# Attention tables, value products and result transfers moved to other places in a hand-scheduled gated mix

## The chip, the cores and the metric

The kernel runs on one core of one Trainium2 chip. The metric is the device time of one execution in microseconds (us), and lower is better. A run's time is a little longer than the span in its trace, which goes from the first to the last instruction.

## What is computed

```python
def _A_ref(x, wqkv, wo):                       # sliding-window attention
    H = 32; Dh = D // H; W = 256               # x: 1 x 2048 x 512, so Dh = 16
    q, k, v = ...(x @ wqkv)...
    scores = einsum("bhqd,bhkd->bhqk", q, k) * (Dh ** -0.5)
    mask = (idx[:, None] - idx[None, :] >= 0) & (idx[:, None] - idx[None, :] < W)
    p = softmax(where(mask, scores, -1e9))
    return merge_heads(einsum("bhqk,bhkd->bhqd", p, v)) @ wo

def _B_ref(x, w1, b1, w2, b2):                 # dense MLP, F = 1792
    return gelu(x @ w1 + b1) @ w2 + b2

g = sigmoid((x * gate_w).sum(-1, keepdims=True))
return g * _A_ref(x, wqkv, wo) + (1 - g) * _B_ref(x, w1, b1, w2, b2)
```

All inputs and the output are float32. The kernel reaches that precision by splitting operands of its dense products into a high and a low part and adding three products (`mm3`: high x high, high x low, low x high).

## The kernel before, in words

The 2048 rows of x are cut into four parts of T = 512 rows (index `t` or `c`), each of four blocks of 128 rows. One Python generator, `dense()`, walks the dense work in order: Q, K and V of the four parts (`qkv`), eight MLP turns (`mlp`: four parts times two halves of the hidden width; each turn has a stage `u`, x @ w1 with the GELU, and a stage `y`, h @ w2), and at the end the output projection (`final`). A second loop walks attention. It has 128 steps `u`, each one block of 128 keys of one of eight groups of four heads. `m = u + LEAD` runs 12 blocks ahead and computes the row maxima (`att_max`, line 519 with its reduction on VectorE, line 524), and `att_exp` computes the scores again with the maxima subtracted (line 564), their exponentials on ScalarE (line 586), and POOL's selects that cut out what lies outside the window (line 580; in the last 12 blocks VectorE does this, line 574). In each step four such pairs of score products alternate with dense work, which `fill` draws from the generator by a share of STEP = 2330 ns of its own cost model.

`att_pvs` multiplies probabilities and values (line 608). It does nothing but in every fourth block: there it multiplies all six blocks that one part of queries sees, into two PSUM buffers which it takes from the same rings of three as the score products (tags `st` and `sm`). ScalarE and VectorE evacuate them (lines 629, 632). In the program before, `att_pvs(u - 1)` stands in step `u` after the score products of `i == PVAT == 2`; in the last 12 steps it stands at the end of the step, and the very last comes during the output projection (`HELD`). After it in a step come the loads `load_ks` and, by `att_load_v` (line 505), of the next values into one of two buffers that earlier value products read.

Each engine runs its instructions in the order in which the program issues them. That order is made with a clock of the program's own: `after(ns, fn)` puts a piece of work into a heap, `tick(ns)` moves the clock and issues what is due. Engines wait for one another through semaphores alone, so a due time sets the place in an engine's queue, and not a time on the chip.

All transfers are issued from SP's queue. At the start, `qkv(0)` loads the rows of x and all weights of Q, K, V. The first weights are copied to their high part by POOL (`split_now`, line 194), and their low part is made by VectorE; later weights get a high part from ScalarE (line 178) and a low part from POOL or VectorE (line 182). Before that, POOL fills the tables: `mask`, `cut`, `own`, `nil`, `nms` and the end of `vbuf` (lines 75 to 102). The second half of the MLP's turns writes its results to DRAM (`YB`); `load_y` (line 848) fetches those of three parts back near the end of attention, into space that the operands of the maxima gave up, six transfers placed YGAP apart. In `final`, `scale_y` multiplies them by 1 - g, `end` adds the projected attention times g (line 879) and stores 128 rows of the output (line 883).

The program reserves 256 bytes per partition for descriptors of GpSimd's queue (`dynamic_dma_scratch_size=256`); nothing uses that queue before the change.

Of the kernel before, what the change touches and what calls it, by code (L numbers as in the profile page):

```python
# [13 lines left out]
ALU = mybir.AluOpType  # L14
# [5 lines left out]
NT = S // T  # L20
NB = T // 128
# [5 lines left out]
NEG = -1e30  # L27
# [5 lines left out]
def gated_mix(ctx: ExitStack, tc: tile.TileContext, x, wqkv, wo, w1, b1, w2, b2, gate_w, out):  # L33
    nc = tc.nc
    x = x[0]
    out = out[0]
# [9 lines left out]
    def f32(ap):  # L46
        return ap.bitcast(F32)
# [24 lines left out]
    make_identity(nc, ident)  # L72
    gwb = sb.tile([128, D], F32, tag="ya", bufs=2, name="gwb")
    b1c = cs.tile([128, NF], F32, name="b1c")
    nc.gpsimd.memset(mask, 0.0)
    for r in (0, 64):
        nc.gpsimd.affine_select(out=mask[r:r + 64, 0:64], in_=mask[r:r + 64, 0:64], pattern=[[1, 64]],
                                compare_op=ALU.is_ge, fill=NEG, base=-1, channel_multiplier=-1)
        nc.gpsimd.affine_select(out=mask[r:r + 64, 256:320], in_=mask[r:r + 64, 256:320], pattern=[[-1, 64]],
                                compare_op=ALU.is_ge, fill=NEG, base=0, channel_multiplier=1)  # L80

    cut = cs.tile([128, 2, 64], F32, name="cut")
    nc.gpsimd.memset(cut, 3e38)
    for r in (0, 64):
        for e in (0, 1):
            v = cut[r:r + 64, e]
            nc.gpsimd.affine_select(out=v, in_=v, pattern=[[1 - 2 * e, 64]], compare_op=ALU.is_ge, fill=0.0,
                                    base=-e, channel_multiplier=2 * e - 1)

    own = cs.tile([128, 4], F32, name="own")  # L90
    nil = cs.tile([128, 1], F32, name="nil")
    nc.gpsimd.memset(nil, 0.0)
    nc.gpsimd.memset(own, 0.0)
    for s in (0, 1):
        for k in (0, 1):
            v = own[64 * s:64 * s + 4].rearrange("r (p s) -> r s p", s=2)[:, s]
            nc.gpsimd.affine_select(out=v, in_=v, pattern=[[-2, 2]], compare_op=ALU.not_equal,
                                    fill=1.0, base=-k, channel_multiplier=1)
    nms = cs.tile([128, 2 * RB, 32], F32R, name="nm")
    nc.gpsimd.memset(f32(nms), 0.0)  # L100
    vbuf = cs.tile([128, 2, NB * 68 + 16], F32, name="vbuf")
    nc.gpsimd.memset(vbuf[:, :, NB * 68:], 0.0)
    z = cs.tile([128, S // 128], F32, name="z")
    g = cs.tile([128, S // 128], F32, name="g")
    g1 = cs.tile([128, S // 128], F32, name="g1")

    def mm3(p, lh, ll, rh, rl, first, last):
        nc.tensor.matmul(p, lh, rh, start=first, stop=False)  # L108
# [82 lines left out]
    def split_now(key, copy, eng):  # L191

        w = sb.tile([128, 2, T], F32R, tag="w", bufs=14, name=f"qk_{key[1]}")
        copy(w[:, 0], raws[key])
        eng.tensor_sub(w[:, 1], raws.pop(key), f32(w[:, 0]))
        wt[key] = w.rearrange("p s (c f) -> p s c f", c=NC)
        done.add(("w", key))
# [172 lines left out]
    def qkv(t):  # L370
        last = t == NT - 1
        qk = [("qk", j) for i in range(NC) for j in (i, i + NC)]
        vs = [("v", b) for b in range(NB)]
        pieces = qk[:4] + vs + qk[4:] if last else qk + vs
        if t == 0:
            keys = qk + [("v", c) for c in range(NC)]
            load_xr(0, (0, 1))
            load_raw(keys[0], True)
            load_xr(0, (2, 3))
            for key in keys[1:]:  # L380
                load_raw(key, True)
            nc.sync.dma_start(gwb, gate_w.partition_broadcast(128))
            warm(WARM[0])
            qkv_x(0, 0), qkv_x(0, 1)
            split_now(keys[0], nc.gpsimd.tensor_copy, nc.vector)
            warm(WARM[1])
            p = [ps.tile([128, T], F32, tag="d", bufs=2, name=f"qk0_{n}") for n in range(2)]
            j0, j1 = keys[0][1], keys[1][1]
            yield qk_half(p[0], j0, 0, [(0, 0)])
            qkv_x(0, 2)  # L390
            yield qk_half(p[0], j0, 0, [(0, 1), (1, 0)])
            split_now(keys[1], lambda o, i: nc.scalar.activation(o, i, AF.Copy), nc.vector)
            qkv_x(0, 3)
            parts = [(0, 0), (0, 1), (1, 0)]
            yield qk_half(p[1], j1, 0, parts)
            yield qk_half(p[0], j0, 1, parts)
            qk_out(0, j0, p[0])
            yield qk_half(p[1], j1, 1, parts)
            qk_out(0, j1, p[1])
        need(*[("x", t, b) for b in range(NB)])  # L400
        for n, (kind, j) in enumerate(pieces):
            if not last and XAT <= n < XAT + NC:
                nc.sync.dma_start(XT[t][n - XAT], f32(xts[t][:, n - XAT]))
            if kind == "qk":
                need(("w", (kind, j)))
            else:
                need(*[("w", ("v", c)) for c in range(NC)])
            if t == 0 and n == 10:
                nc.sync.dma_start(b1c, b1.rearrange("(f p) -> p f", p=128))
            if t == 0 and n < 2:  # L410
                pass
            elif kind == "qk":
                yield from qkv_qk(t, j)
            else:
                yield from qkv_v(t, j)
            if t == 1 and n % 3 == 2:
                clear_k(n // 3)
            if t == 2 and n < 4:
                clear_q(n)
            if t == 2 and n in (1, 2):  # L420
                load_kd(0, n - 1)
            if t == 2 and n in (8, 9):
                load_ks(0, n - 8)
            if t == 0:
                for i in ([2], [3], [4], [5], [6], [7, 8], [9, 10], [11])[n] if n < 8 else []:
                    split(keys[i], nc.vector if i % 2 else nc.gpsimd)
                if n == 1:
                    after(4000, gate, 0)
                    after(4000, load_xr, 1)
            elif n == 0 and not last:  # L430
                load_xr(t + 1)
            if last and n not in (6, 7):
                load(later.pop(0))
            if last and n == len(pieces) - 1:
                for _ in range(4):
                    load(later.pop(0))
            xat = (5, 7, 8, 9) if t == 0 else (4, 6, 8, 10)
            if not last and n in xat:
                qkv_x(t + 1, xat.index(n))
            if not last and n == xat[-1] + 1:  # L440
                gate(t + 1)
# [399 lines left out]
    def load_y(t, i):  # L841

        need(*[("y", 1, t, b) for b in range(NB)])
        if t < 2:
            v = f32(qd[:, t, i]).rearrange("p (j f) -> p j f", j=2)
        else:
            v = f32(kd[:, i, :, 0:T])
        nc.sync.dma_start(v, YB[t].rearrange("(i j p) f -> i p j f", j=2, p=128)[i])
        for j in range(2):
            ybs[t * NB + 2 * i + j] = v[:, j]  # L850

    def scale_y(nb, a):
# [4 lines left out]
    def final(t):  # L857
# [16 lines left out]
        def end(b, k, cs):  # L874
            nb, a, p = t * NB + b, parts[b], parts[b, k]

            def ev():
                need(("yb", nb))
                nc.vector.scalar_tensor_tensor(a[:, cs], p, g[:, nb:nb + 1], a[:, cs],
                                               op0=ALU.mult, op1=ALU.add)  # L880

            def store():
                nc.sync.dma_start(out[nb * 128:(nb + 1) * 128, cs], a[:, cs])
            after(100, ev), after(100 + (HOLDO if nb < NT * NB - 2 else 800), store)

        turns = [(b, c) for b in range(NB) for c in range(NC)]
# [50 lines left out]
    NU = NG * NKB  # L937
# [5 lines left out]
    for u in range(-LEAD, NU):  # L943
# [3 lines left out]
        for i in range(4):  # L947
            if i == 1 and m % NB == 0 and NB <= m < NU - NB:
                load_kd(*divmod(m // NB + 1, NT)), load_qd(*divmod(m // NB + 1, NT))
            if i % 2 == 0:  # L950
                pair = (i, i + 1) if stage[0] != "u" else (i,)
            elif len(pair) == 2:
                continue
            else:
                pair = (i,)
            for op, i in [(op, k) for k in pair for op in ORDER[:3]] + [("f", k) for k in pair]:
                if op == "s" and u >= 0:
                    att_exp(u // NKB, u % NKB, i)
                if op == "m" and m < NU:
                    att_max(gm, bm, i ^ XOR)  # L960
                if op == "p" and i == PVAT and 1 <= u <= NU - LEAD:
                    att_pvs(u - 1)
                if op == "f":
                    fill(step / 4)
        if m < NU and bm % RB == RB - 1:
            after(900, att_rows, gm, bm // RB)
        if m % NB == QAT % NB and QAT <= m < QAT + NKB:
            load_qs(0, (m - QAT) // NB)
        if u > NU - LEAD:
            att_pvs(u - 1)  # L970
        if u % NB == 0 and NB <= u < NU - NB:
            load_ks(*divmod(u // NB + 1, NT))
# [43 lines left out]
MXAT = 5500.0  # L1016
AHEAD = 9e3
STEP0 = 2750.0
PVAT = 2
HELD = 2  # L1020
YAT = 5
YGAP = 2500
STEP = 2330.0
_TC = dict()
_INS = ["A_x", "A_wqkv", "A_wo", "B_w1", "B_b1", "B_w2", "B_b2", "gate_w"]
# [18 lines left out]
```

## Time and profile before

| | |
|---|---|
| median of 3 runs | 751.1 us (749.64 to 757.67) |
| profiled execution | 749.65 us, span 747.9 us |
| TensorE (PE) busy | 732.7 us, 98% of the span |
| VectorE (DVE) busy | 520.1 us, 70% |
| ScalarE (ACT) busy | 421.5 us, 56% |
| GpSimd (POOL) busy | 372.3 us, 50% |
| transfers | 172.12 MB, mean 230 GB/s, all on SP's queue |
| granted TensorE clock | 1.00 |

In the rows of the profile, PE is TensorE's matrix work and PEld its weight loads, SPq is the issue of transfers on SP. "L608" is line 608 of the kernel. "pt<-st" names the tile written and the tile read. A wait is put down to what came last. The ends of matmuls are modelled, so a busy TensorE can hide short waits inside a run of matmuls; they show as a larger step between two starts.

### The profile page before, as it was taken

How to read it: one execution, taken by the hardware profiler on the slowest of the kernel's cores; microseconds unless marked ns; L12 is line 12 of the kernel's file. 1: busy time of each engine (PE TensorE's matmuls, PEld its weight loads, DVE VectorE, ACT ScalarE, POOL GpSimd, SP SyncE). 2: the span in 40 equal slices, each digit the busy share in tenths (PEclk: the TensorE clock that was granted, in tenths of full speed). 3: DMA queues.
4: the chain of work that ended last, by engine and by line, in shares of the span. 5: the costliest groups of instructions: out<-in, count | busy, mean ns of one | idle time of the engine just before them, and what ended most of it. 6: DMA issues, size and time to landing. Idle time of an engine off the chain costs nothing.

```text
span 747.9 us, 17961 instructions
## 1 busy us (share of the span) xinstructions
PE 732.7 (98%) x6129; PEld 604.4 (81%) x6129; DVE 520.1 (70%) x1567; ACT 421.5 (56%) x972; POOL 372.3 (50%) x846
## 2 busy tenths in 40 slices
PE   8999999998999999999999999999999999999998
PEld 7888888876788888888887877888888888867786
DVE  4532325799768867986798689768867986784552
ACT  4434532358537845864695478438745863794550
POOL 4200000339756865876577568747765875630000
PEclk9999999999999999999999999999999999999999
DMA  9889798998895687899575979996799799468572
GB/s 326 319 272 404 261 391 273 291 293 182 270 259 134 162 243 205 175 222 271 146 179 149 242 211 234 249 237 152 178 256 235 194 224 270 136 181 226 191 252 111
DMA packets 179260, 172.12 MB, mean 230 GB/s; under 512 B 56673, under 2 KB 122977, under 8 KB 179169
## 3 DMA queue, kind: packets, MB, share of 16 engines
q1 hardware_dynamic: 179168, 170.97, 81.4%
q8 instruction: 49, 0.80, 0.5%
q14 instruction: 43, 0.34, 0.1%
HBM read 108.53 MB, written 62.39 MB: 229 GB/s over the span
## 4 chain that ended last, share of the span: by engine, by line
PE 85%; DVE 5%; ACT 3%; issue 3%; DMA 2%; SPq 1%; POOL 1%; DVEq 0%; ACTq 0%
PE sm L519 9%; PE st L564 8%; PE pv_sm L608 7%; PE y L108 7%; PE y L109 6%; PE y L110 6%; PE u L108 5%; PE u L109 5%; PE u L110 5%; PE qk L110 4%; PE qk L108 4%; PE qk L109 4%; PE a L108 2%; DVE jm L524 2%; PE v L108 2%
## 5 line engine op out<-in xcount | busy, mean ns | idle before, releaser
L524 DVE CUSTOM_DVE_ANT_0 jm<-sm,mask 128x320 bf16<-128x320 f32 (+4 forms) x512 | 238.1, 465 | 95.3 <-PE sm L519 61.1
L580 POOL TENSOR_SCALAR_AFFINE_SELECT pt<-pt 64x256 f32<-64x256 f32 (+1 forms) x538 | 227.7, 443 | 108.5 <-ACT pt L586 98.1
L586 ACT ACTIVATE pt<-st 128x320 f32<-128x320 f32 (+4 forms) x512 | 199.6, 424 | 139.1 <-PE st L564 136.0
L519 PE MATMUL sm<-kd,qd 96*128 96x320 f32 (+4 forms) x512 | 153.9, 312 | 6.3 <-DVE M L524 5.5
L564 PE MATMUL st<-qs,ks 128*128 128x320 f32 (+4 forms) x512 | 153.9, 309 | 1.9 <-ACT pt L586 1.9
L546 POOL CAST qs<-tt 4x256 fp32r<-4x256 f32 x256 | 124.6, 487 | 53.3 <-DVE tt L539 42.7
L519 PEld LDWEIGHTS sm<-kd,qd 96*128 96x128 f32 x512 | 96.3, 188 | 33.2 <-DVE M L524 13.7
L564 PEld LDWEIGHTS st<-qs,ks 128*128 128x128 f32 x512 | 97.1, 190 | 18.8 <-ACT pt L586 3.2
L108 PE MATMUL y<-w,h 128*128 128x512 f32 x224 | 88.5, 395 | 0.0
L109 PE MATMUL y<-w,h 128*128 128x512 f32 x224 | 87.9, 393 | 0.0
L110 PE MATMUL y<-w,h 128*128 128x512 f32 x224 | 87.9, 392 | 0.0
L108 PE MATMUL u<-mx,w 128*128 128x512 f32 x196 | 80.0, 408 | 0.0
L109 PE MATMUL u<-mx,w 128*128 128x512 f32 x196 | 77.4, 395 | 0.0
L110 PE MATMUL u<-mx,w 128*128 128x512 f32 x196 | 77.1, 393 | 0.0
L608 PE MATMUL pv_sm<-pt,vbuf 64*32 64x320 f32 (+4 forms) x1408 | 73.6, 346 | 0.2
L608 PE MATMUL pv_st<-pt,vbuf 64*32 64x320 f32 (+4 forms) x1408 | 73.3, 346 | 0.0
L608 PEld LDWEIGHTS pv_sm<-pt,vbuf 64*32 64x32 f32 x1408 | 50.2, 106 | 20.2 <-issue 2.4
L325 DVE TENSOR_TENSOR qke<-qk,qke 128x512 fp32r<-128x512 f32 x32 | 22.0, 688 | 46.9 <-ACT qke L322 33.2
L322 ACT ACTIVATE qke<-qk 128x512 fp32r<-128x512 f32 x32 | 19.1, 597 | 56.2 <-PE qk L110 32.5
L110 PEld LDWEIGHTS y<-w,h 128*128 128x128 f32 x224 | 42.0, 188 | 9.8
L338 POOL MEMSET vx<- 128x32 f32 x16 | 2.4, 156 | 89.0 <-DMA SQ<-qke 44.5
L608 PEld LDWEIGHTS pv_st<-pt,vbuf 64*32 64x32 f32 x1408 | 46.1, 106 | 0.0
(148 smaller groups left out, 1332.7 us busy)
## 6 DMA issues: line engine op xcount, KB each, us to landing
kd<-SK SPq DMA_DIRECT2D x32, 384.0 KB
qs<-SQ SPq DMA_DIRECT2D x64, 192.0 KB
mx<-XT SPq DMA_DIRECT2D x24, 512.0 KB
SQ<-qke SPq DMA_DIRECT2D x16, 512.0 KB
SK<-qke SPq DMA_DIRECT2D x16, 512.0 KB
ND<-nd SPq DMA_DIRECT2D x32, 256.0 KB
raw_w<-in_B_w_dram SPq DMA_DIRECT2D x28, 256.0 KB
ks<-SK SPq DMA_DIRECT2D x32, 192.0 KB
```

The costliest lines, as they stand in the source:

```text
L108: nc.tensor.matmul(p, lh, rh, start=first, stop=False)
L109: nc.tensor.matmul(p, lh, rl, start=False, stop=False)
L110: nc.tensor.matmul(p, ll, rh, start=False, stop=last)
L322: nc.scalar.activation(e[:, h], p, AF.Copy)
L325: nc.vector.tensor_sub(e[:, 1 - h], p, f32(e[:, h]))
L519: nc.tensor.matmul(p[:, :w], qd[0:96, n, pr, 128 * j:128 * (j + 1)], kd[0:96, n, pr, k1 - w:k1], start=True, stop=True)
L524: nc.vector.tensor_tensor_reduce(junk[:, :w], p[:, :w], mask[:, 320 - w:320], 1.0, -3e38, ALU.add, ALU.max, M[:, 2 * (b % RB) + hb, pr:pr ...
L546: nc.gpsimd.tensor_copy(dst, src.unsqueeze(1).broadcast_to([4, 2, RB, 32]))
L564: nc.tensor.matmul(p[:, :w], ks[:, slot(g_, kb // NB), pr, at:at + 128], qs[:, pr, k0:k0 + w], start=True, stop=True)
L580: nc.gpsimd.affine_select(out=v, in_=v, pattern=[[0, v.shape[1]], [1 - 2 * e, 64]], compare_op=ALU.is_ge, fill=0.0, base=-e, channel_multi ...
L586: nc.scalar.activation(pt[:, hf, pr, :w], p[:, :w], AF.Exp, scale=SCALE)
L608: nc.tensor.matmul(pv[r // 64][32 * i:32 * i + 32, q - c * T:e - c * T], vts[g_, b // NB][r:r + 64, v:v + 32], rhs(r), start=start, stop=s ...
```

## The change

There are five edits.

1. The tables' 18 POOL instructions move into a function `tables()`, called in `qkv(0)` behind `split_now(keys[0], ...)`. Only the identity and the tile `idle` stay in front.
2. The split of the third weights (`keys[2]`) is issued during the first two half products, and the list of later splits moves up by one place.
3. All value products stand at the end of their step, behind its dense work; `PVAT` goes.
4. `load_y` issues its transfers on GpSimd's queue, each in two halves of 256 KB, and YGAP is 4500 in place of 2500.
5. The output's stores go over GpSimd's queue, but for the last two blocks.

```diff
+    def tables():
+        nc.gpsimd.memset(mask, 0.0)
...
+        nc.gpsimd.memset(f32(nms), 0.0)
+        nc.gpsimd.memset(vbuf[:, :, NB * 68:], 0.0)
...
             split_now(keys[0], nc.gpsimd.tensor_copy, nc.vector)
+            tables()
             warm(WARM[1])
...
             yield qk_half(p[1], j1, 0, parts)
+            split(keys[2], nc.gpsimd)
             yield qk_half(p[0], j0, 1, parts)
...
-                for i in ([2], [3], [4], [5], [6], [7, 8], [9, 10], [11])[n] if n < 8 else []:
+                for i in ([3], [4], [5], [6], [7], [8], [9, 10], [11])[n] if n < 8 else []:
                     split(keys[i], nc.vector if i % 2 else nc.gpsimd)
...
-        nc.sync.dma_start(v, YB[t].rearrange("(i j p) f -> i p j f", j=2, p=128)[i])
         for j in range(2):
+            nc.gpsimd.dma_start(v[:, j], YB[t].rearrange("(i j p) f -> i p j f", j=2, p=128)[i][:, j])
             ybs[t * NB + 2 * i + j] = v[:, j]
...
             def store():
-                nc.sync.dma_start(out[nb * 128:(nb + 1) * 128, cs], a[:, cs])
+                queue = nc.gpsimd if nb < NT * NB - 2 else nc.sync
+                queue.dma_start(out[nb * 128:(nb + 1) * 128, cs], a[:, cs])
...
-                if op == "p" and i == PVAT and 1 <= u <= NU - LEAD:
-                    att_pvs(u - 1)
                 if op == "f":
                     fill(step / 4)
...
-        if u > NU - LEAD:
+        if u >= 1:
             att_pvs(u - 1)
...
-PVAT = 2
-YGAP = 2500
+YGAP = 4500
```

More of the change, by code (lines that the diff above doesn't have):

```diff
@@ L74, in gated_mix @@
     b1c = cs.tile([128, NF], F32, name="b1c")
[L75 to L80, printed above, removed]
-    cut = cs.tile([128, 2, 64], F32, name="cut")
[L83 to L88, printed above, removed]
+    cut = cs.tile([128, 2, 64], F32, name="cut")
     own = cs.tile([128, 4], F32, name="own")
     nil = cs.tile([128, 1], F32, name="nil")
[L92 to L98, printed above, removed]
     nms = cs.tile([128, 2 * RB, 32], F32R, name="nm")
-    nc.gpsimd.memset(f32(nms), 0.0)
     vbuf = cs.tile([128, 2, NB * 68 + 16], F32, name="vbuf")
-    nc.gpsimd.memset(vbuf[:, :, NB * 68:], 0.0)
     z = cs.tile([128, S // 128], F32, name="z")
@@ L105, in gated_mix @@
     g1 = cs.tile([128, S // 128], F32, name="g1")
+    def tables():
+        nc.gpsimd.memset(mask, 0.0)
+        for r in (0, 64):
+            nc.gpsimd.affine_select(out=mask[r:r + 64, 0:64], in_=mask[r:r + 64, 0:64], pattern=[[1, 64]],
+                                    compare_op=ALU.is_ge, fill=NEG, base=-1, channel_multiplier=-1)
+            nc.gpsimd.affine_select(out=mask[r:r + 64, 256:320], in_=mask[r:r + 64, 256:320], pattern=[[-1, 64]],
+                                    compare_op=ALU.is_ge, fill=NEG, base=0, channel_multiplier=1)
+        nc.gpsimd.memset(cut, 3e38)
+        for r in (0, 64):
+            for e in (0, 1):
+                v = cut[r:r + 64, e]
+                nc.gpsimd.affine_select(out=v, in_=v, pattern=[[1 - 2 * e, 64]], compare_op=ALU.is_ge, fill=0.0,
+                                        base=-e, channel_multiplier=2 * e - 1)
+        nc.gpsimd.memset(nil, 0.0)
+        nc.gpsimd.memset(own, 0.0)
+        for s in (0, 1):
+            for k in (0, 1):
+                v = own[64 * s:64 * s + 4].rearrange("r (p s) -> r s p", s=2)[:, s]
+                nc.gpsimd.affine_select(out=v, in_=v, pattern=[[-2, 2]], compare_op=ALU.not_equal,
+                                        fill=1.0, base=-k, channel_multiplier=1)
+        nc.gpsimd.memset(f32(nms), 0.0)
+        nc.gpsimd.memset(vbuf[:, :, NB * 68:], 0.0)
     def mm3(p, lh, ll, rh, rl, first, last):
```

## The prediction

> **What bounds the kernel now.** I read the page first, then the table of windows, then the timeline of the first microseconds, and last the chain of waits at single places.
>
> ```profile
> span 747.9 us, 17961 instructions
> PE 732.7 (98%) x6129; PEld 604.4 (81%) x6129; DVE 520.1 (70%) x1567; ACT 421.5 (56%) x972; POOL 372.3 (50%) x846
> PE 85%; DVE 5%; ACT 3%; issue 3%; DMA 2%; SPq 1%; POOL 1%; DVEq 0%; ACTq 0%
> ```
>
> TensorE is the bound: 732.7 of 747.9 us busy and 85% of the chain that ended last. The change removes no matmul, so it can win only time in which TensorE stands: 747.9 - 732.7 = 15.2 us shown as idle, and some waits inside a run of matmuls that the modelled ends hide. Where the idle time lies (start:end and length, PE busy, then PEld, DVE, ACT, POOL, clock, share of the DMA engines, GB/s):
>
> ```profile
> 0.00:13.00 13.00, 10.77 (x75) 9.18 (x76) 4.25 (x7) 5.00 (x8) 5.07 (x26) 1.00 0.90 292
> 13.00:25.00 12.00, 11.57 (x52) 8.86 (x51) 9.11 (x17) 5.33 (x12) 3.85 (x3) 1.00 0.76 279
> 25.00:75.00 50.00, 50.00 (x235) 41.35 (x234) 16.98 (x34) 20.48 (x53) 3.78 (x10) 1.00 0.96 352
> 150.00:200.00 50.00, 46.18 (x320) 36.80 (x326) 44.76 (x136) 33.72 (x72) 33.91 (x66) 1.00 0.92 247
> 300.00:400.00 100.00, 98.11 (x925) 81.53 (x910) 83.52 (x262) 69.20 (x157) 72.13 (x158) 1.00 0.79 194
> 400.00:500.00 100.00, 98.21 (x972) 79.93 (x972) 78.93 (x256) 56.91 (x134) 67.15 (x155) 1.00 0.90 228
> ```
>
> 2.2 us lie in the first 13 us, 0.4 in the next 12, 3.8 at 150 to 200 (VectorE 44.76 of 50 us busy there, a limit that the change leaves alone), 1.9 and 1.8 in the two hundreds, the rest near the end. The clock is granted in full throughout.
>
> **Part 1, the start.** The rows read: start, duration, engine, line, operation; in brackets what ended the idle time before.
>
> ```profile
> 0.81 0.87 SPq L245 DMA_DIRECT2D xr<-in_A_x_dram  x2
> 1.62 0.36 POOL L75 MEMSET mask<- 128x320 bf16 x1
> 1.72 0.43 SPq L170 DMA_DIRECT2D raw_qk<-in_A_wqkv_dram  x1
> 3.60 1.37 PE L261 MATMUL xp<-ident,xr 128*128 128x128 f32 x8
> 4.57 1.09 ACT L265 ACTIVATE ks<-xp 128x512 fp32r<-128x512 f32 x2 [2.48 <-PE xp L261]
> 5.67 0.12 POOL L102 MEMSET vbuf<- 128x32 f32 x1
> 5.86 0.61 POOL L194 CAST qk<-raw_qk 128x512 fp32r<-128x512 f32 x1
> 6.52 0.73 PE L310 MATMUL qk<-ks,qk 128*128 128x256 f32 x4 [1.01 <-POOL qk L194]
> 13.20 0.28 PE L310 MATMUL qk<-ks,qk 128*128 128x256 f32 x1
> 13.28 1.28 POOL L182 TENSOR_TENSOR qk<-raw_qk,qk 128x512 fp32r<-128x512 f32 x1 [6.81 <-DMA raw_v<-in_A_wqkv_dram]
> 13.55 0.47 PE L108 MATMUL qk<-ks,qk 128*128 128x512 f32 x1
> 14.61 0.50 PE L110 MATMUL qk<-ks,qk 128*128 128x512 f32 x1 [0.36 <-POOL qk L182]
> 14.95 0.39 PE L108 MATMUL qk<-ks,qk 128*128 128x512 f32 x1
> 23.02 0.19 PEld L110 LDWEIGHTS qk<-ks,qk 128*128 128x128 f32 x1 [0.37 <-DVE qk L182]
> ```
>
> POOL builds its tables from 1.62 to 5.79 us and only then copies the first weights; the first product waits for that copy (6.52). With the tables behind it, the copy waits for its transfer alone. The first x block was issued at 0.81 and is read at 3.60, so 2.8 us later at most; the raw weights, issued at 1.72, are then there by about 4.5, the copy runs to 5.1 to 5.3, and the next that is late is ScalarE's copy of the second x block, done at 4.57 + 1.09 = 5.66. The first product starts at about 5.72: 0.80 us won (bounds: 0, if the weights land as late as now, and 0.86, if it starts in the moment ScalarE is done).
>
> The tables then hold POOL until 5.3 + 4.17 = 9.5 us. Behind them stands POOL's low part of the third weights (L182), which now is issued one product earlier; it takes 1.28 us, so to about 10.8, while the product that reads it begins at 13.5 - 0.8 = 12.7. Now that low part starts at 13.28 because its copy on ScalarE stands behind the first product's output. The three first matmuls of this product take from 13.55 to 14.95 = 1.40 us, while the window from 25 to 75 us has 235 matmuls in 50 us, 0.21 each: 0.7 us won, and another 0.2 before them, where the last half product starts at 13.20 and the next matmul only at 13.55. All later low parts are issued one product earlier too, which takes away the 0.37 us at 23.02 (0.2 of it beyond the usual pace). Sum 0.8 + 0.7 + 0.2 + 0.2 = **1.9 us**. The tables' first readers are the maxima and the clearing of `ks` in the second x part, past the 25 us of these rows. The 25 to 75 us window, with its engines 0.96 full, asks whether the transfers can follow 1.9 us earlier; TensorE has 50.00 of 50 us there, so no transfer is late now. I keep the 1.9; zero is the lower bound.
>
> **Part 2, the values' products.** Now they come after the third of four score pairs of a block, then the fourth pair and half a block of dense work; afterwards they come behind all of it. 29 of the 32 move (the last three stand so already); nothing is added. What they gain is time for what they wait for, POOL's selects and ScalarE's exponentials of the block before. Places where that wait shows (the first lines TensorE, the POOL lines from the chain):
>
> ```profile
> 232.13 0.64 POOL pt L580
> 232.54 0.22 PE L608 MATMUL pv_st<-pt,vbuf 64*32 64x64 f32 x2
> 232.82 0.25 PE L608 MATMUL pv_sm<-pt,vbuf 64*32 64x64 f32 x2
> 382.57 0.36 PE L564 MATMUL st<-qs,ks 128*128 128x320 f32 x1
> 383.60 0.30 PE L608 MATMUL pv_st<-nil,vbuf 64*32 64x64 f32 x2 [0.66 <-ACT pt L586]
> 604.72 0.71 POOL pt L580
> 605.13 0.22 PE L608 MATMUL pv_st<-pt,vbuf 64*32 64x64 f32 x2
> 605.48 0.25 PE L608 MATMUL pv_sm<-pt,vbuf 64*32 64x64 f32 x2
> ```
>
> At 232 the products run on only when the select ends (232.77): 0.3 us. At 605 the same: 0.35. At 383 they wait 0.8 us for an exponential and lose 0.2 more. Together 1.65, with smaller ones 1.8 us. The move gives them half a block's dense share, 1,165 ns by the constant STEP, and a score pair: longer than each of these waits, so they go. I take **1.8 us** (bounds: 1.8 won, and 10.2 lost, if each of the 29 met one wait of 0.35 at its new place; I stay at the first, since what they read is only older there).
>
> What comes later: the next score products need PSUM buffers. The change puts two score pairs between the value products and the buffers that they gave up, so the evacuation by ScalarE and VectorE has the same distance as now; I cost it at nothing, covered by a fill of dense work.
>
> On SP the load of the next values' block (L505) waits for these products, as it overwrites what they read:
>
> ```profile
> SPq L505 <- PE st L564: 10.9, 9, 3.7
> SPq L505 <- PE pv_sm L608: 6.6, 4, 2.1
> ```
>
> From 200 to 600 us SP stood 17.5 us there, up to 3.7 at once. The products end about 1.5 us later, 29 times, so up to 44 us more of SP's standing; behind it wait weights, x parts and stores. The weights have 7.5 us of lead by the constant LAND, and transfers are 2% of the chain over the whole span: 0, with an upper bound of 0.25 us each, 7.3 us.
>
> **Part 3, GpSimd's queue.** The rows: POOL's last work, SP's loads of the MLP's results, VectorE's outputs, SP's stores, its last wait, and a long transfer.
>
> ```profile
> 659.72 3.07 POOL L546 CAST qs<-tt 4x256 fp32r<-4x256 f32 x5
> L848 SPq DMA_DIRECT2D qd<-YB x4: 433/458/469, 663.3 to 669.2; - x4
> 703.76 0.74 DVE L879 SCALAR_TENSOR_TENSOR ao<-a,g,ao 128x512 f32<-128x512 f32 x1
> 738.05 1.43 DVE L879 SCALAR_TENSOR_TENSOR ao<-a,g,ao 128x512 f32<-128x512 f32 x2 [3.34 <-PE a L110]
> L883 SPq DMA_DIRECT2D out_dram<-ao x17: 332/333/430, 707.1 to 745.3; - x17
> SPq L1040 <- DMA out_dram<-ao: 1.2, 1, 1.2
> 433.07 7.66 DMA rb<-RD
> ```
>
> POOL has nothing after 662.8 us. Its queue gets 12 loads (each of six split in two) and 14 stores of 256 KB; the last two blocks' stores stay on SP. No load waits for anything by then, so they follow each other from about 663 at POOL's own pace, whatever YGAP says. If one takes s us, POOL is through with the loads at 663.3 + 12s and with the stores at the largest of 663.3 + 26s, 704.5 + 14s (the first output is there at 704.5) and 738.8 + 2s (the last two, at 738.05 + 0.75). The kernel's last store lands at about 747. So POOL decides only from **s = 3.04 us** on. No row shows a transfer on POOL. Bounds: 0.33 us (SP's issue) and 7.66 us (a transfer's whole way in a crowded stretch, if only one may be under way). Nearest is the last store, issued at 745.3 and waited for 1.2 us beyond its 0.33, so 1.5 for 128 KB; 128 KB more at the page's mean 230 GB/s add 0.57: s = 2.1, which ends at 743.0. Cost **0**. The first output (703.76) needs the first of the loads, which is there at 665.4. The late YGAP and SP's freed slots gain nothing, as TensorE waits for no store or load here.
>
> The Trainium skill, page "DMA: Bandwidth & Descriptors", section "Anatomy of one DMA — SWDGE (gpsimd) path", gives such a transfer 2.0 us plus its bytes at 436 GB/s: an estimate of 2.6 us, by which the sum stays the same. The same page says that these descriptors lie in a ring in SBUF; the kernel sets 256 bytes for it, which by the page's 16-byte descriptors and nine of them per engine for 128 rows holds one transfer at a time. The page "SBUF — State Buffer" (section "SBUF: two separate sides") adds that VectorE's two-port operations lock GpSimd out of writing them. No run here shows either; they speak for the slower rival.
>
> **The sum.** 1.9 + 1.8 = 3.7 us off the profiled execution's 749.65 us (1.75 us of it outside the span): 745.95. The median of the runs shown is 751.1, 1.45 above it, so I forecast 751.1 - 3.7 = **747.4 us**.
>
> **The rivals.**
> - *The start's gain is swallowed.* If the transfers at 0.96 of their engines cannot move up, TensorE stands 1.9 us later instead. Against it: nothing waits there now. Only 1.8 remain: 749.3 us.
> - *It gains more.* While the value products run, VectorE and ScalarE starve; with a full block's scores and dense outputs given out before, they work on through them, and the 1.9 + 1.8 us idle in the 300 to 500 us windows, where VectorE is 79 to 84% busy, go as well. For it: those stalls lie in VectorE's busiest windows after 200 us. Against: most are not near a value product. 747.4 - 3.7 = 743.7; a little more, from the busy 150 to 200, gives 743.
> - *GpSimd's queue decides (slower).* If it takes one transfer at a time and s is over 3.04, the stores are the end. At s = 4 they end at 663.3 + 104 = 767.3 with 0.9 us of closing behind: 768.2 against 747.9, and the loads start 3.7 earlier: +16.6, so 767.7 us. At 3.5 it is 3.6 us over before, 754.7. For it: transfers of up to 7.66 us in the trace.
> - *SP is late.* SP's upper bound of part 2, 7.3 us on the forecast: 754.7 us. Against it: SP stands there already without harm.
>
> **How the numbers follow.** Forecast 0.42, swallowed 0.12, more gain 0.22, GpSimd's queue 0.14, SP late 0.10. A measurement here tells about 1% (7.5 us) from nothing. Faster by over 1% (under 743.6) is the third case, 0.22; slower (over 758.6) the fourth but for its mild end, and the worst of the fifth with part 2's other bound, 0.17; within 1% the rest, 0.61. The forecast's own range is 744 to 750. The range leaves out the larger part of the fourth case and the best of the third, and reaches up to part 2's far bound, 747.4 + 10.2: **741.5 to 757.5**.
>
> **What would show it.** Right: the copy L194 starts near 4.6 and the first L310 product near 5.7; the product's matmul now at 14.95 comes near 13.2; POOL's L182 starts near 9.5. The value products follow a dense matmul without a gap, and the chain no longer runs through POOL's selects. POOL's transfers follow at 2 to 3 us, the last by 743, and the chain still ends over TensorE, VectorE and SP. Wrong: a TensorE gap at 30 to 120 us that ends with a transfer; a store on POOL landing last; SP standing over 3 us at L505 with TensorE waiting for weights; or the value products' waits coming back.

## The result: 1.1% slower, and the profile after

The changed kernel takes 758.42 us (median of nine runs, 757.05 to 761.91) against 750.47 us, a ratio of 1.0111 with a 95% interval of 1.0092 to 1.0129. The forecast was 747.4 us, with a range of 741.5 to 757.5. The profiled execution took 758.78 us with a span of 757.1 us, 9.2 us more than before. From the page:

```profile
span 757.1 us, 17997 instructions
PE 735.2 (97%) x6129; PEld 602.7 (80%) x6129; DVE 518.7 (69%) x1567; ACT 421.0 (56%) x972; POOL 385.7 (51%) x872
...
q0 software_dynamic: 2080, 6.82, 2.7%
...
PE 76%; issue 10%; DVE 5%; DMA 4%; ACT 2%; POOL 1%; SPq 1%; POOLq 0%; DVEq 0%; ACTq 0%
```

TensorE's share of the chain that ended last fell from 85 to 76%; "issue" rose from 3 to 10%, and q0 is GpSimd's queue, unused before. The windows (start:end and length, PE busy, then PEld, DVE, ACT, POOL, clock, DMA share, GB/s) tell where:

```profile
0.00:13.00 13.00, 11.13 (x71) 9.27 (x72) 3.96 (x6) 5.22 (x9) 6.98 (x27) 1.00 0.90 277
13.00:25.00 12.00, 12.00 (x58) 9.87 (x57) 9.55 (x17) 5.69 (x12) 3.87 (x4) 1.00 0.85 302
...
300.00:400.00 100.00, 98.29 (x954) 80.45 (x954) 83.19 (x262) 68.38 (x157) 71.57 (x158) 1.00 0.78 195
400.00:500.00 100.00, 98.14 (x974) 79.71 (x975) 78.07 (x256) 56.76 (x135) 66.86 (x155) 1.00 0.89 224
...
686.00:701.00 15.00, 13.00 (x147) 10.04 (x129) 7.07 (x15) 6.60 (x18) 1.64 (x3) 1.00 0.74 216
701.00:720.00 19.00, 17.07 (x161) 13.30 (x159) 7.40 (x13) 8.30 (x14) 2.72 (x5) 1.00 0.72 218
720.00:757.10 37.10, 29.60 (x132) 24.29 (x132) 14.38 (x23) 8.84 (x15) 6.01 (x11) 0.95 0.46 164
```

The first 25 us have less idle time than before, the middle is as it was, and all of the loss lies behind 686 us. The same is read from single matmuls: for the n-th matmul that writes a given tile, its start in one trace minus its start in the trace of before. This is TensorE's lag (minus: ahead), in us, at five places; the last column is the time from the start of the last matmul to the end of the span. The kernels below the second row are experiments, told further down. A trace is of one execution, and not always of a middling one: that of e6_pv115 took 750.65 us (median 748.53), that of e14_ring115 748.48 (median 753.93).

| kernel | 25 us | 375 us | 680 us | 702 us | 735 us | last matmul to end |
|---|---|---|---|---|---|---|
| before | 0 | 0 | 0 | 0 | 0 | 3.5 |
| changed | -0.6 | +0.3 | -1.3 | +1.1 | +7.0 | 5.6 |
| e1_sp | -1.2 | -0.3 | -2.4 | +3.4 | +4.5 | 3.5 |
| e2_gponly | +0.1 | +0.2 | +0.7 | +0.7 | +6.1 | 10.7 |
| e6_pv115 | -0.2 | +2.8 | +0.5 | +0.5 | +0.9 | 3.5 |
| e11_pvonly | +0.1 | +1.0 | -1.6 | +3.2 | +4.3 | 3.5 |
| e12_both115 | +0.1 | +1.2 | -1.1 | -1.1 | +1.3 | 12.6 |
| e14_ring115 | -1.2 | -0.4 | -2.6 | -2.6 | -1.5 | 3.8 |

The changed kernel is 1.3 us ahead at 680 us. Then it loses 2.4 near 690, 5.9 near 720 and 2.1 after the last matmul: -1.3 + 2.4 + 5.9 + 2.1 = 9.1 us. What ends those waits (engine, line, what it waited for: us in total, times, longest; 680 us to the end):

```profile
ACT ot L709 <- DMA ot<-OT: 17.9, 5, 6.7
...
POOL out_dram L887 <- issue: 15.7, 5, 4.9
...
DVE den L653 <- DMA den<-ND: 7.5, 3, 5.3
...
ACT nd L632 <- DMA OT<-num: 5.6, 1, 5.6
```

The first wait of TensorE ends with ScalarE's `nd`, which waits for the store OT<-num; the second hangs on VectorE, where an output's evacuation stands behind the reciprocal (L653), which waits for den<-ND:

```profile
692.05 0.74 PE L567 MATMUL st<-qs,ks 128*128 128x320 f32 x2 [2.00 <-ACT nd L632]
...
719.20 0.35 DVE L653 RECIPROCAL den<-den 128x32 f32<-128x32 f32 x1 [5.26 <-DMA den<-ND]
...
722.01 0.50 PE L109 MATMUL a<-wo,ot 128*128 128x512 f32 x1 [3.94 <-DVE ao L882]
...
722.67 0.63 PE L111 MATMUL a<-wo,ot 128*128 128x512 f32 x1
723.10 0.63 PE L109 MATMUL a<-wo,ot 128*128 128x512 f32 x1
...
725.66 0.49 PE L109 MATMUL a<-wo,ot 128*128 128x512 f32 x1
```

Both belong to the same kind of chain. Each of the last group's four parts goes through DRAM three times: ND<-nd and den<-ND; after the reciprocal RD<-den and the loads num and rb; after their product OT<-num and ot<-OT. The last fence also shows a second price of a stall: the matmuls behind it step by 0.43 us instead of 0.23, seven times, some 1.4 us more; the granted clock is 0.50 from 722.5 to 725.6 us.

POOL's transfers, first and last of loads and stores:

```profile
661.89 0.70 POOL L852 DMA_DIRECT2D qd<-YB  x1
665.33 0.55 POOL L852 DMA_DIRECT2D qd<-YB  x1 [2.74 <-issue]
...
707.30 0.54 POOL L852 DMA_DIRECT2D kd<-YB  x1 [3.93 <-issue]
710.45 0.55 POOL L887 DMA_DIRECT2D out_dram<-ao  x1 [2.60 <-DVE ot L712]
...
741.50 0.55 POOL L887 DMA_DIRECT2D out_dram<-ao  x1 [2.02 <-DVE ao L882]
744.06 0.54 POOL L887 DMA_DIRECT2D out_dram<-ao  x1 [2.02 <-issue]
...
753.73 0.54 POOL L887 DMA_DIRECT2D out_dram<-ao  x1 [2.03 <-issue]
```

From 661.89 to 753.73 there are 26 transfers, one each (753.73 - 661.89) / 25 = 3.67 us, and never under 2.56 us. The loads, all issued by 677.46 us in the kernel before, go on to 707.30 among the last round trips, and the stores queue behind the loads. The queue never pauses: each of the 25 later transfers is issued 0.30 to 0.32 us after the one before it has landed. And the chain that ended last runs from 690 us to the end over these transfers and the waits between them alone; two of its rows:

```profile
744.07 0.54 POOL out_dram L887
744.60 2.00 issue
```

So in the changed kernel GpSimd's queue sets the end, and TensorE's stalls lie beside it.

### The profile page after: what moved, and what is told of

Read it like the earlier page. It is cut to its first block, busy times and chain, and to the rows that moved or that the text cites. A ratio compares the mean times of both kernels' runs of the same rounds, so it can differ in the third digit from the quotient of the medians.

```text
span 757.1 us, 17997 instructions
## 1 busy us (share of the span) xinstructions
PE 735.2 (97%) x6129; PEld 602.7 (80%) x6129; DVE 518.7 (69%) x1567; ACT 421.0 (56%) x972; POOL 385.7 (51%) x872
## 4 chain that ended last, share of the span: by engine, by line
PE 76%; issue 10%; DVE 5%; DMA 4%; ACT 2%; POOL 1%; SPq 1%; POOLq 0%; DVEq 0%; ACTq 0%
PE sm L522 10%; PE st L567 8%; PE pv_sm L611 7%; PE y L109 6%; PE y L110 6%; PE y L111 6%; PE u L109 5%; PE u L110 5%; PE u L111 5%; PE qk L109 4%; PE qk L111 4%; PE qk L110 4%; DVE jm L527 2%; PE v L109 2%; PE v L111 2%
## 5 line engine op out<-in xcount | busy, mean ns | idle before, releaser
L589 ACT ACTIVATE pt<-st 128x320 f32<-128x320 f32 (+4 forms) x512 | 197.2, 423 | 122.6 <-PE st L567 118.8
L632 ACT ACTIVATE nd<-pv_st 128x512 f32<-128x512 f32 x32 | 19.1, 597 | 62.4 <-PE pv_sm L611 51.6
```

Of the source, the lines that this page charges most:

```text
L589: nc.scalar.activation(pt[:, hf, pr, :w], p[:, :w], AF.Exp, scale=SCALE)
```

## The experiments

My theory at first was GpSimd's queue for all of the loss; the rival was the value products' move.

### Which part loses: both queues back on SP, and the queue alone

e1_sp is the changed kernel with

```diff
-            nc.gpsimd.dma_start(v[:, j], YB[t]...[i][:, j])
+        nc.sync.dma_start(v, YB[t]...[i])
...
-                queue = nc.gpsimd if nb < NT * NB - 2 else nc.sync
-                queue.dma_start(out[nb * 128:(nb + 1) * 128, cs], a[:, cs])
+                nc.sync.dma_start(out[nb * 128:(nb + 1) * 128, cs], a[:, cs])
...
-YGAP = 4500
+YGAP = 2500
```

> The changed kernel with the loads of the MLP's results and all stores back on SP's queue (one transfer a load, YGAP 2500): what is left is the tables' move, the earlier split and the value products' move. Theory (GpSimd's queue takes one transfer at a time; its backlog and its traffic make SP's last chain late): up to 686 us the changed kernel's trace ran 1.3 us ahead of the one before, and nothing after that is disturbed, so about 749.3 us, 0.2% under before. Rival (the value products at the end of their block make SP's loads and the denominators' chain late): the TensorE stalls of 2.2 and 4.3 us near 690 and 720 us stay, and the time is about 756 us.

Measured: 754.71 us, 1.0052 (1.0038 to 1.0067). The theory, that the queue is all of it, falls; without anything on GpSimd's queue the kernel is already 0.5% slower, as the rival said. The waits near 690 us:

```profile
ACT nd L632 <- DMA OT<-num: 7.0, 1, 7.0
...
PE st L567 <- ACT nd L632: 3.5, 1, 3.5
```

e2_gponly is the kernel before with the opposite of that diff.

> The kernel before with edits 4 and 5 alone: loads in halves and most stores on GpSimd's queue, YGAP 4500; tables and value products as before. Theory (GpSimd's queue): the whole loss and none of the 1.3 us won, so about 758.4 + 1.3 = 759.7 us, with the stalls near 690 and 720 us and the last store on POOL landing last. Rival (value products): only the 2.2 us of late stores at the end stay, about 752.7 us.

Measured: 762.54 us, 1.0151 (1.0127 to 1.0176). So the queue loses too, 1.5% on the kernel before (11.5 us, 2.8 more than the theory had), and 0.6% on top of the other edits (1.0111 against 1.0052). The two losses overlap. POOL's first store is issued at 718.59, its last at 757.94.

e3_loads and e4_stores are the changed kernel with only the stores, or only the loads, back on SP.

> The changed kernel with the stores back on SP; only the loads of the MLP's results go over GpSimd's queue. Theory, if the loads are what makes SP's chain late (they run from 662 to 710 us, when SP's chain falls behind): the stalls near 690 and 720 us stay, 2.2 late at the end goes, about 749.3 + 6.5 = 756 us. If the stores' backlog is what costs: POOL is free after about 710 us and SP stores, about 749.5 us. Rival (value products): 756 us as well, but then the kernel with both on SP shows it too.

> The changed kernel with the loads back on SP (one transfer each, YGAP 2500); only the stores of the first 14 blocks go over GpSimd's queue. Theory, if the loads make the loss: the stores start at 704.5 us, at 2.6 us each they are done by 741, and nothing waits, about 749.5 us. If the stores need 3.7 us each (the mean spacing of POOL's transfers in the changed kernel): 704.5 + 14 x 3.7 = 756 us for the last, about 758 us in all.

Measured: 757.67 us, 1.0080 (1.0066 to 1.0094), and 757.68 us, 1.0082 (1.0069 to 1.0096). Against e1_sp each costs 0.3%, and both together 0.6%. The intervals are too wide to say which costs more; with either of them TensorE's stalls near 690 and 720 us stay.

### Which edit brings the stall near 690 us: tables alone, value products alone, all but one of them

e5_tables is the kernel before with edits 1 and 2; e11_pvonly has edit 3 alone.

> The kernel before with edits 1 and 2 alone (tables behind the first copy, third weights' split earlier). In the run with both queues on SP, TensorE was 1.2 us ahead at 25 us. Theory (the denominators' chain of transfers through DRAM is only just in time for TensorE near 690 us in the kernel before): TensorE keeps the lead and gives a little of it back near 690 us, 750.0 to 750.6 us against 751.0. Rival (the chain is a hard bound): the whole lead turns into a stall near 690 us, 751.0 us or more.

> The kernel before with edit 3 alone: all value products at the end of their block, block 115's too. Theory (its later place puts the last group's chain about 4 us later, and TensorE waits for it whenever it arrives): the same end as with the tables, 754.5 to 755.5 us. Rival (it costs only because the tables' move brings TensorE there earlier): 752 to 753 us.

Measured: 750.35 us, 0.9998 (0.9984 to 1.0012), and 754.59 us, 1.0049 (1.0027 to 1.0071). The tables' move is worth nothing that can be measured; the value products' move is the whole loss of e1_sp, with the tables in front or behind.

Why? The value products of the last group are those of blocks 115, 119, 123 and 127, and only the first of these is among the 29 that moved. (The last three stood behind their dense work already.) Its chain is now half a block late in the program beside the unmoved work of the next ones. SP's rows of before, then of e1_sp:

```profile
681.49 0.61 SPq L646 DMA_DIRECT2D den<-ND  x1
...
682.22 0.37 SPq L665 DMA_DIRECT2D OT<-num  x1
682.64 1.40 SPq L703 DMA_DIRECT2D ot<-OT  x3
```

```profile
683.10 0.61 SPq L649 DMA_DIRECT2D den<-ND  x1
683.75 1.40 SPq L706 DMA_DIRECT2D ot<-OT  x3
...
686.02 0.36 SPq L668 DMA_DIRECT2D OT<-num  x1
...
692.06 0.60 ACT L632 ACTIVATE nd<-pv_st 128x512 f32<-128x512 f32 x1 [7.04 <-DMA OT<-num]
```

OT<-num, which stood ahead of three `ot` loads, now stands behind them, and den<-ND ahead of both is later too; OT<-num is issued 3.8 us later. The tile `nd` of block 123 takes the buffer (one of three of the ring `tmp`) that this store reads, ScalarE waits for it, and TensorE waits for the PSUM buffer that ScalarE would free. e6_pv115 is e1_sp with one exception:

```diff
+                if op == "p" and i == PVAT and u == NU - LEAD:
+                    att_pvs(u - 1)
...
-        if u >= 1:
+        if u >= 1 and u != NU - LEAD:
```

> The changed kernel with both queues back on SP, and one value product of the 29 moved ones, that of block 115, back at its old place behind the third score pair. Its result starts the last group's chain of denominators; of the four chains of that group it is the only one whose start had moved. Theory (moving that start by half a block put OT<-num behind three ot loads in SP's order, from 682.2 to 686.0 us, and TensorE waits for it through ScalarE's nd): the 5.5 us lost near 690 us go, about 754.7 - 4.5 = 750.2 us or less. Rival (all moved value products make SP's loads late, or the loads of the MLP's results do it): nothing changes, 754.7 us.

Measured: **748.53 us, 0.9977 (0.9964 to 0.9990)**, 0.75% (5.6 us) under e1_sp, and 0.2% under the kernel before. One value product out of 29 was the loss of e1_sp. SP has its old order again:

```profile
681.98 0.61 SPq L649 DMA_DIRECT2D den<-ND  x1
...
682.73 0.36 SPq L668 DMA_DIRECT2D OT<-num  x1
...
683.45 1.41 SPq L706 DMA_DIRECT2D ot<-OT  x3
...
690.08 0.60 ACT L632 ACTIVATE nd<-pv_st 128x512 f32<-128x512 f32 x1 [2.46 <-PE pv_sm L611]
```

### Is it the buffer or the chain?

e7_ndraw is e1_sp with a free buffer for that one `nd`:

```diff
+        tag, bufs = ("raw", 2) if u == NU - 5 else ("tmp", 3)
-        nd = sb.tile([128, T], F32, tag="tmp", bufs=3, ...)
+        nd = sb.tile([128, T], F32, tag=tag, bufs=bufs, ...)
```

> The changed kernel with both queues back on SP; the evacuation tile nd of block 123 gets a buffer of the ring raw, which is free by then, instead of the ring tmp whose buffer OT<-num still reads. The order of the transfers stays. Theory (TensorE waits near 690 us for the score products' PSUM buffer, whose evacuation waits for the store OT<-num to be done with its buffer): the stall of 3.5 us and the slower clock behind it go; the late chain may cost up to 2 us more near 717 us: 749.5 to 752 us. Rival (what is late is the chain as such): 754.7 us.

Measured: 755.87 us, 1.0071 (1.0054 to 1.0088). My theory fell and the rival held: the wait for OT<-num near 690 us is gone, and the same time is lost a little later: 1.7 us near 696, where TensorE waits for ScalarE, and 5.4 near 720, where the chain arrives just as late (the last part's reciprocal starts at 717.75, in e1_sp at 718.34, in the kernel before at 712.97). The row of that `nd`, and then the waits from 680 to 760 us:

```profile
688.06 0.60 ACT L633 ACTIVATE nd<-pv_st 128x512 f32<-128x512 f32 x1 [2.46 <-PE pv_sm L611]
```

```profile
DVE den L654 <- DMA den<-ND: 8.8, 3, 5.3
...
PE a L109 <- DVE ao L883: 3.6, 2, 3.5
```

The buffer was where the late chain showed first, not the cause.

e15_later (e1_sp) and e16_later115 (e6_pv115) make the loads of the MLP's results due 3 us later:

```diff
-                after(1500 + YGAP * k, load_y, *divmod(k, 2))
+                after(4500 + YGAP * k, load_y, *divmod(k, 2))
```

> The changed kernel with both kinds of transfers on SP (754.7 us), and the first load of the MLP's results due 3 us later by the program's clock: den<-ND of block 115's chain now stands ahead of all these loads, while OT<-num still stands behind three ot loads. Theory (the place of OT<-num behind the ot loads costs most of the 5.5 us): the reciprocal comes 2 us earlier, near 668.5, but TensorE still waits near 690 us, 753 to 754.7 us. Rival (the load ahead of den<-ND costs most): the stall near 690 us goes, 749 to 751 us.

> The kernel with block 115's value product back and both kinds of transfers on SP (748.5 us), with the same later loads. There neither load stands ahead of den<-ND nor ot loads ahead of OT<-num. Theory: the chain was in time already, 747.5 to 749.5 us. Rival (later loads crowd the later round trips): a stall near 717 us, 751 us or more.

Measured: 754.30 us, 1.0053 (1.0035 to 1.0071), and 750.35 us, 1.0001 (0.9990 to 1.0013). So the load ahead of den<-ND isn't what costs: e15_later came as the theory said. But I had also expected the reciprocal 2 us earlier, and it is not. The rows of e15_later:

```profile
662.20 0.63 SPq L649 DMA_DIRECT2D den<-ND  x1
...
669.86 0.69 DVE L728 SCALAR_TENSOR_TENSOR sqh<-sqh,x1h 128x512 f32<-128x512 f32 x1
670.46 0.35 DVE L653 RECIPROCAL den<-den 128x32 f32<-128x32 f32 x1
```

The reciprocal follows the row before it without a wait: VectorE's order, too, holds it half a block back (668.43 in the kernel before). No run separates what SP's order costs from what VectorE's does. e16_later115 lies between its theory and its rival, 0.24% over e6_pv115. Its trace, of the slowest of ten executions (752.47 us), shows the rival's stall: 4.0 us are lost near 720 us. So loads among the last round trips seem to cost time on SP's queue too, less than on GpSimd's.

### GpSimd's queue on a kernel whose chain is in time

e9_loads115, e10_stores115 and e12_both115 are e6_pv115 with the loads, the stores, or both on GpSimd's queue; the last is the changed kernel with block 115 back.

> The kernel with tables, value products but block 115's, and stores on SP, which ran at 748.5 us; now the loads of the MLP's results go over GpSimd's queue (12 halves, 256 bytes of descriptors, YGAP 4500). Theory (the queue takes one transfer at a time, so the loads run on until about 710 us, in the middle of the last round trips through DRAM, and make them late): a TensorE stall near 717 us like the 5.5 us with the queue alone, 753 to 754.5 us. Rival (the stores alone cost): 748.5 us.

> As the kernel at 748.5 us, with the loads on SP and only the stores of the first 14 blocks on GpSimd's queue. Theory: POOL begins with the first output near 705 us; 14 stores at 2.57 us end by 745, the last ones follow the last outputs, so only the pair at the end is late, 1 to 2 us: 749.5 to 751 us. Rival (stores on GpSimd's queue slow the round trips as much as the loads do): a stall of 3 us or more near 717 us, 753 us or more.

> The changed kernel with all edits, loads and stores on GpSimd's queue, and only the value product of block 115 back at its old place. Theory if the two losses are separate: 758.4 - 6.2 = 752.2 us. Theory if both use up the same slack, the time by which the last chain through DRAM is ahead of TensorE: the loads and stores alone make it late, as they did on the kernel before (762.5), so 757 to 760 us, no better than the changed kernel.

Measured: 752.03 us, 1.0020 (0.9996 to 1.0043); 752.70 us, 1.0027 (1.0011 to 1.0043); 758.90 us, 1.0105 (1.0078 to 1.0133). Beside 0.9977 the loads cost 0.43%, the stores 0.50%, both 1.28%, more than their sum by these figures, though the intervals leave room for no difference. The traces of the first two lose 3.0 us (loads) and 0.9 us (stores) near 720 us, and the stores 2.7 us more behind the last matmul; 752.70 lies between that run's theory and its rival. Block 115 brings nothing on the changed kernel, as the second theory said, though not for the reason I gave. TensorE loses 2.4 us near 720 us there, and then the end waits for POOL:

```profile
752.42 0.56 POOL L887 DMA_DIRECT2D out_dram<-ao  x1 [2.02 <-issue]
754.99 0.54 POOL L887 DMA_DIRECT2D out_dram<-ao  x1 [2.01 <-issue]
```

The last matmul starts 12.6 us before the end. So the queue alone brings the whole loss, and the late chain lies hidden beside it: without the chain the queue's limit stays, and without the queue (e1_sp) the chain's.

### One transfer at a time?

e8_ring (e2_gponly), e13_ring (the changed kernel) and e14_ring115 (e12_both115) have room for more descriptors:

```diff
-dynamic_dma_scratch_size=256
+dynamic_dma_scratch_size=512
-    cut = cs.tile([128, 2, 64], F32, name="cut")
+    cut = cs.tile([128, 2, 64], BF16, name="cut")
```

> The kernel before with edits 4 and 5 alone and 512 instead of 256 bytes for the descriptors of GpSimd's queue (the table cut is kept as bf16 to make the room). Theory (one transfer at a time fits, and each new one waits until the one before is through): the stores' smallest distance of 2.57 us falls to about half, the last store is no longer late, 762.5 - 7 = 755.5 us or less. Rival (a fixed cost of POOL for each transfer): the distance stays 2.57 us and the time 762.5 us.

> The changed kernel with all edits and 512 instead of 256 bytes for the descriptors of GpSimd's queue (cut as bf16). Theory (with one transfer at a time POOL's 26 transfers set the end, and the late chain of block 115 lies hidden under them): the queue's limit goes and the late chain is left, as with both kinds on SP: 754 to 756 us. Rival (the transfers slow the chain through DRAM whatever their order): 757 to 759 us.

> The same with 512 bytes, and the value product of block 115 back at its old place. Theory: both causes gone, 748.5 to 751 us. Rival: 753 us or more, a stall near 717 us as in the kernel before with the queue alone and 512 bytes (755.0 us).

Measured: 755.03 us, 1.0050 (1.0031 to 1.0069); 756.42 us, 1.0088 (1.0067 to 1.0109); 753.93 us, 1.0029 (1.0003 to 1.0056), with single times from 747.72 to 755.64. (One further run of e14_ring115 took 1446.82 us, which no trace shows and the ratio leaves out.) POOL's rows of e13_ring, its first and last transfers, and then its largest wait:

```profile
661.40 1.76 POOL L852 DMA_DIRECT2D qd<-YB  x3
...
673.74 0.54 POOL L852 DMA_DIRECT2D kd<-YB  x1 [0.78 <-issue]
...
744.70 1.22 POOL L887 DMA_DIRECT2D out_dram<-ao  x2 [4.15 <-DVE ao L882]
```

```profile
POOL out_dram L887 <- DVE ao L882: 63.9, 13, 35.5
```

The time of e13_ring lies near the theory's 754 to 756 us; that of e14_ring115 missed its theory (748.5 to 751). Three transfers are issued in 1.76 us, the last load at 673.74 and not at 707.30, the stores follow their outputs, and the last matmul is 3.8 us from the end. So the spacing of 2.56 us and more was no fixed cost of POOL but the ring with its place for one transfer. In all seven kernels with 256 bytes each transfer waits until the one before has landed (2.2 to 6.9 us after its issue); with 512 bytes it no longer does. The whole grid:

| | SP | GpSimd, 256 bytes | GpSimd, 512 bytes |
|---|---|---|---|
| block 115 moved | 1.0052 | 1.0111 | 1.0088 |
| block 115 back | 0.9977 | 1.0105 | 1.0029 |

With the larger ring block 115 is worth 0.6% again. What stays open is the 0.4 to 0.5% by which 512 bytes still lose against SP. The trace of e14_ring115 is of an execution of 748.48 us that loses 1.1 us near 720 us; that of e8_ring has 4.9 us near 720 us. I take it for the same round trips, in time in one execution and not in the next, but no run separates that.

## Why the prediction was wrong, point by point

**The start: right in kind, mis-sized.** I put the first weights' arrival at 4.5 us, from the time another transfer took, and won 0.8 us by it, 1.9 in all. In the traces with this edit the copy still waits for its weights, and starts between these two (e1_sp, e12_both115), in the changed kernel at 6.26:

```profile
5.05 0.61 POOL L195 CAST qk<-raw_qk 128x512 fp32r<-128x512 f32 x1 [3.38 <-DMA raw_qk<-in_A_wqkv_dram]
```

```profile
7.00 0.61 POOL L195 CAST qk<-raw_qk 128x512 fp32r<-128x512 f32 x1 [5.32 <-DMA raw_qk<-in_A_wqkv_dram]
```

In nine of the fourteen traces that is later than the 5.86 us of before: the weights are the limit then, not the tables, and my lower bound of zero was the nearer one. In three kernels whose tables are still in front (e2_gponly, e8_ring, e11_pvonly) the copy waits for its weights too, 0.17 to 0.51 us. The other terms came: TensorE's lag falls by 0.7 us between 12 and 16 us, and the 0.37 us at 23.02 went. The changed kernel's lead is 0.6 us at 25 us, and by 375 us it is gone.

**The value products' waits: right.** They went: from 200 to 680 us TensorE's wait at a value product for an exponential (0.66 us at 383; the 0.8 of my sum is more than the row shows) is gone, and the chain that ended last no longer runs over POOL's selects. Between 375 and 680 us the lag falls by 1.6 to 2.6 us wherever the products moved (table). From 25 to 680 us it falls by 0.7 to 1.7 us, but for the trace of e6_pv115, which loses 3 us before 375; 1.8 was forecast.

**The value products' consequences: one of the two steps that failed.** I asked what stands behind these products on TensorE (nothing that waits) and on SP (L505, bound 7.3 us), but not what they issue: their evacuation, the store ND and the denominators' chain are due relative to them, and those of block 115 moved against three that did not. "SP is late" named 754.7 us; e1_sp and e11_pvonly came at 754.7 and 754.6. The time agrees by luck, the mechanism doesn't: it is the order of one chain on SP and VectorE, not a wait for vbuf. SP did stand longer at the loads of the values (30.1 us behind TensorE from 200 to 600 us in e1_sp, 18.7 before), but no wait of TensorE there ends with a transfer.

**GpSimd's queue: the other step that failed, and the dearer one.** I put its cost at 0, with s = 2.1 us from the last store on SP, where several transfers may be under way; measured is 2.56 at least and 3.67 in the mean, above the 3.04 from which POOL was to decide. It costs 1.28% with block 115 in place (e12_both115 against e6_pv115), and the rival had its mechanism. At 3.67 the formula gives 663.3 + 26 x 3.67 = 758.7, and the span ended at 757.1. The estimate of 2.6 us by the Trainium skill (page "DMA: Bandwidth & Descriptors", section "Anatomy of one DMA — SWDGE (gpsimd) path") agrees with the smallest spacing. What neither value had is that a transfer takes longer to land among SP's traffic, with up to 6.7 us to the next one. What I did not have at all is that loads stretched to 707 us meet the last round trips.

**The other rivals.** The start's gain was swallowed, in e5_tables by the median all of it: in part by the weights' arrival, and in that trace the 0.7 us left at 160 us go at a wait of 2.04 us for VectorE at 163 us. No transfer at 30 to 120 us is in it. More was not gained: the idle time at 300 to 500 us stayed: 98.29 and 98.14 of 100 us busy, 98.11 and 98.21 before.

## What to carry to other kernels

When a step moves, list what it issues and what is due relative to it, and look for the one whose neighbours did not move; the end of a pipeline, where a chain of round trips through DRAM arrives just in time, is where half a block shows as several us. A queue is priced by how many transfers it can hold under way, not by the time to issue one. And when undoing one suspect brings nothing, a second limit may lie just behind it: undo both.

## What the runs showed of the hardware

TensorE's clock drops after a stall, and the stall need not be long. Behind 3.94 us of waiting in the changed kernel seven matmuls stepped by 0.43 us at a granted clock of 0.50, and behind 2.12 us in e16_later115 the step was 0.43 us as well, while the 2.00 us near 692 in the changed kernel left it at 0.23 and the clock at 1.00. The Trainium skill, page "TensorE: Matmul & The Clock Gate", section "Part 1: The HAM clock gate (the "warmup" mystery)", puts the slow rate at half the clock, 426.7 ns for 512 columns, after an idle window of about 3.4 us that runs on its own. The rate agrees; the runs met it after shorter waits than that.

A transfer of 256 KB on GpSimd's queue occupies POOL for 0.54 us. With 256 bytes of descriptors per partition the next was issued only 0.30 to 0.32 us after the one before had landed: another 2.0 us at least, and up to 6.2 us in the changed kernel while SP's transfers were under way. With 512 bytes three went out in 1.76 us.
